# Turning the attention output of 17 chunks by way of the chip's memory in four transfers, in place of eight direct ones

## The chip, the cores and the metric

One NeuronCore of a Trainium2 chip runs the whole kernel. The metric is the device time of one execution in microseconds (us), lower is better. Every time below is from runs of the kernel before, or from the hardware profile of one of its executions.

## The reference

The kernel computes three layers one after the other. A gated linear attention over 4 sequences of 768 tokens, 8 heads of width 48, whose state runs along the tokens; a dense layer 384 to 2048 to 384 with x·sigmoid(x) between; and a layer of 8 experts in which every token goes to the one expert that its logits prefer.

```python
for t in range(S):
    state = f[:, :, t, :, None] * state + np.einsum('bhd,bhe->bhde', k[:, :, t], v[:, :, t])
    y[:, :, t] = np.einsum('bhd,bhde->bhe', q[:, :, t], state)
x = y.transpose(0, 2, 1, 3).reshape(B * S, H * D)
h = x @ w_in
x = (h * (1.0 / (1.0 + np.exp(-h)))) @ w_out
...
h = np.maximum(xe @ w1[e], 0.0)
out[mask] = gate_w[mask, None] * (h @ w2[e])
```

All inputs and outputs are f32; there are 3072 tokens of 384 values.

## The kernel before, in words

The 3072 tokens are 24 chunks of 128. The attention of a chunk is done in closed form with matmuls, and the state is carried from chunk to chunk. The chunks make nine groups of the dense layer (2, 2, six times 3, and 2 chunks): group 3 is chunks 7 to 9, group 4 chunks 10 to 12, group 5 13 to 15, group 6 16 to 18, group 7 19 to 21, group 8 22 and 23. A group has 16 slots. In slot i, `moe_h` multiplies the group's tokens with 128 columns of w_in into a bank `ph` (9 matmuls on x split into a high part `xth` and a low part `xtl`), ACT makes `se` (a tanh), DVE makes `sg` from both, and `moe_g` splits that into `gh` and `gl`; two slots later (`LAG`, L85) `moe_o` multiplies these with w_out into `px`. There are two `ph` banks, so the `ph` of slot i+2 needs the `sg` of slot i. In a group's first slot the matmuls on `xth` come ahead of those on `xtl` (L673).

The attention of later chunks is spread over the slots of the group before theirs: `s0 = pos[g, 0] - NF + r * NF // sizes[g] - ASH` (L1338) and `S1` (L80) put a chunk's six stages into slots. For the last chunk of a group of three the stage that makes `xth` and `xtl` (`x_high`, `x_low`, L642 and L647) falls into the last slot ahead of the group's own first slot.

The dense layer wants a chunk's attention output transposed, with model columns on the partitions: y as 128 partitions of 3 x 128. From chunk 4 on the attention makes it already transposed, head by head: `y_out` (L576) copies two PSUM banks into a tile `yt` of 112 partitions by 4 by 128 (two heads of 48 rows each on partitions 0 to 47 and 64 to 111, in four column blocks). `y_turn` (L590) rearranges this into the tile `y`: every 16 partitions of `y` take one head's 48 rows, three rows to a partition. For chunks 4 to 6 (`TURN`, L109), whose steps stand in the hand-written list `STEPS` (`yd:4` to `yd:6`), it writes `yt` into a scratch tensor `ys` in the chip's memory with three transfers and reads it back with a fourth. For chunks 7 to 23 it issues eight transfers of 24 KB from tile to tile, one a head. All are issued on SP (`sy.dma_start`). The buffer of `y` is single, that of `yt` one of two under the tag `am`.

From group 2 on only TensorE's order and a few other instructions are kept as written; the rest of the order on SP, ACT, DVE and POOL comes from a scheduler that works with a model of the times. SP's other transfers beside a chunk are the loads of `v`, `q`, `k` and `f` of later chunks (`load_chunk`, L207), the pair `ends` and `a_all`, and a second load of the dense weights (`in_again`, `out_again`). At the end of group 7 SP also loads the first expert's weights (`w_raw`) and the first rows of its tokens (`xe_h`), from which DVE makes the two `oi_h` (L987).

In the profile the turned `y` is read by ACT at L645 (`xth<-y`) and DVE at L649 (`xtl<-y`). In the changed file, lines after L589 are 6 lower.

Of the kernel before, what the change touches and what calls it, by code (L numbers as in the profile page):

```python
# [9 lines left out]
F32 = mybir.dt.float32  # L10
# [11 lines left out]
P = 128  # L22
# [86 lines left out]
TURN = (4, 5, 6)  # L109
# [5 lines left out]
def kernel(  # L115
# [15 lines left out]
    B, H, S, D = q.shape  # L131
# [6 lines left out]
    NPR = H // 2  # L138
    CPB = S // P
    NCH = NT // P  # L140
# [12 lines left out]
    dram = ctx.enter_context(tc.tile_pool(name="dram", bufs=1, space=DRAM))  # L153
# [10 lines left out]

    ends = dram.tile([NCH, DM], F32, name="ends")
    xs = dram.tile([E * CAP, ROW], F32, name="xs")
    ys = {n: dram.tile([NPR * P, P], F32, name=f"ys_{n}") for n in TURN}

    ident = const.tile([P, P], F32, name="ident")
    trir = const.tile([P, P], F32R, name="trir")  # L170
# [15 lines left out]
    zrow = big[:, 4 * DM : 4 * DM + ROW].bitcast(F32)  # L186
    spare = big[:, 5 * DM + 2 : 5 * DM + 3]
    BANKS = {0: "haahhaaa", 1: "-aahhaaa"}

    def turned(n):  # L190
        return n > 6 or n in TURN

    def use(n, i, name):
        if (n, i) in SPARE:
# [12 lines left out]
    def load_chunk(n, names, pin=lambda fn: fn):  # L207
        b, c = divmod(n, CPB)
        g, r = group_of[n]
        for nm in names:  # L210
            src = {"f": f_logit, "q": q, "k": k, "v": v}[nm]
            if nm == "v":
                tag, bufs = ("gl", GB) if n == 1 else ("in_v", 1)
                flat = att.tile([P, H * D + 16], F32, tag=tag, name=f"v_{n}", bufs=bufs)
                if turned(n):
                    nc.gpsimd.memset(flat[:, H * D :], 0.0)
                t = flat[:, : H * D].rearrange("p (h d) -> p h d", h=H)
                loaded[nm, n] = flat
            elif n == 1:
                tag = {"f": "sg", "q": "gh", "k": "gh"}[nm]  # L220
                t = att.tile([P, H, D], F32, tag=tag, name=f"{nm}_{n}", bufs=BUFS[tag])
            elif nm == "f":
                if n in F_HOME:
                    fb[g] = att.tile([P, 1, H, D], F32, tag=F_HOME[n], name=f"f_{n}")
                elif n == starts[g]:
                    fb[g] = att.tile([P, CPG, H, D], F32, tag="in_f", name=f"f_{n}")
                t = fb[g][:, r if g > 1 else 0]
            else:
                t = att.tile([P, H, D], F32, tag="in_" + nm, name=f"{nm}_{n}")
            (pin(nc.sync.dma_start) if not strict else sy.dma_start)(out=t, in_=src[b, :, c * P : (c + 1) * P, :].rearrange("h p d -> p h d"))  # L230
            loaded.setdefault((nm, n), t)
# [13 lines left out]
    ve, ac, sy = Pinned(nc.vector), Pinned(nc.scalar), Pinned(nc.sync)  # L245
# [300 lines left out]
    def y_past(n):  # L546
        qt = bd["qt", n]
        for i in range(NPR):
            r = (0, 2, 1, 3)[i] if turned(n) else i
            for j in range(2):  # L550
                rows = slice(64 * j, 64 * j + D)
                if turned(n):
                    pe.matmul(place(n, r, j), packed_state[rows, r, :], qt[rows, r, :], start=r % 2 == 0, stop=False)
                else:
                    pe.matmul(
                        y_banks(n)[j][:, r * D : (r + 1) * D], qt[rows, r, :], packed_state[rows, r, :D],
                        start=r == 0, stop=False,
                    )
# [31 lines left out]
    def y_turn(n):  # L590
        yt = ysb[n]
        y = ysb[n] = att.tile([P, KC, P], F32, tag="y", name=f"y_{n}")
        if n in TURN:
            rows = ys[n].rearrange("(r p) t -> p r t", r=NPR)
            sy.dma_start(out=rows[:112, :2], in_=yt[:112, :2])
            for k in range(2):
                sy.dma_start(out=rows[64 * (1 - k) : 64 * (1 - k) + D, 2:], in_=yt[64 * k : 64 * k + D, 2:])
            sy.dma_start(out=y, in_=ys[n].rearrange("(h x) t -> h x t", h=H)[:, :D])
            return
        for h in range(H):  # L600
            r, j = divmod(h, 2)
            k = j ^ r // 2
            sy.dma_start(out=y[h * P // H : (h + 1) * P // H], in_=yt[64 * k : 64 * k + D, r])

    def att4(n):
        if n % CPB:
            y_past(n)
        y_own(n)
        if n % CPB < CPB - 1:
            gain(n)  # L610
        y_out(n)
        if turned(n):
            y_turn(n)
        if n % CPB < CPB - 1:
            carry(n, bd.pop(("pu", n)), n % CPB == 0)
# [718 lines left out]
    for n in range(NCH):  # L1334
        g, r = group_of[n]
# [74 lines left out]
    def queue(early):  # L1410
# [3 lines left out]
        f=lambda n: load_chunk(n, "f"), k=lambda n: load_chunk(n, "k"), q=lambda n: load_chunk(n, "q"),  # L1414
# [5 lines left out]
        fk=lambda n: flat(n, "k"), fq=lambda n: flat(n, "q"), kt=lambda n: unflat(n, "k"), qt=lambda n: unflat(n, "q"),  # L1420
        sc=scores, am=mask, pu=gain, st=lambda n: carry(n, bd.pop(("pu", n)), n % CPB == 0), past=y_past, own=y_own,
        y=y_out, yd=y_turn, pt=flip_y, xh=x_high, xl=x_low,
        ends=lambda n: put_ends(n, queue(n == 0)), a=lambda n: spread_ends(n, queue(n == 0)),
        w=lambda n: warm(spare_bank[0], n),
# [101 lines left out]
```

## Time and profile before

| what | us |
|---|---|
| median of 3 runs | 825.18 |
| the three runs | 825.69, 819.7, 825.18 |
| the profiled execution | 824.64 |
| its span, first to last instruction | 822.9 |

The rows further down are from that one execution. Times count from the start of the span. PE is TensorE's matmul, DVE VectorE, ACT ScalarE, SPq the issuing of SyncE: the duration of an SPq row is the time to issue, not the transfer. "[2.84 <-DMA y<-yt]" behind a row is how long its engine had been idle before it and what ended that. The core's mean granted TensorE clock is 0.989 of full speed.

### The profile page before, as it was taken

How to read it: one execution, taken by the hardware profiler on the slowest of the kernel's cores; microseconds unless marked ns; L12 is line 12 of the kernel's file. 1: busy time of each engine (PE TensorE's matmuls, PEld its weight loads, DVE VectorE, ACT ScalarE, POOL GpSimd, SP SyncE). 2: the span in 40 equal slices, each digit the busy share in tenths (PEclk: the TensorE clock that was granted, in tenths of full speed). 3: DMA queues.
4: the chain of work that ended last, by engine and by line, in shares of the span. 5: the costliest groups of instructions: out<-in, count | busy, mean ns of one | idle time of the engine just before them, and what ended most of it. 6: DMA issues, size and time to landing. Idle time of an engine off the chain costs nothing.

```text
span 822.9 us, 15636 instructions
## 1 busy us (share of the span) xinstructions
PE 799.7 (97%) x5831; PEld 750.0 (91%) x5831; DVE 467.7 (57%) x1258; ACT 379.1 (46%) x838; POOL 62.4 (8%) x114
## 2 busy tenths in 40 slices
PE   7999999999999999999999999999999999999994
PEld 4889979989999999999999999999899999989994
DVE  7789986555556555646656556366573426345520
ACT  5465564453453453454345342354473526445520
POOL 2000000001000100100100101001200010111001
PEclk9799999999999999999999999999999999999998
DMA  9566686424333343343443422323380617644500
GB/s 217 150 167 161 171 242 183 112 40 116 79 87 90 92 100 83 92 107 78 107 97 79 106 58 57 119 65 119 129 278 31 205 51 259 219 151 161 172 17 29
DMA packets 173197, 100.34 MB, mean 122 GB/s; under 512 B 115507, under 2 KB 166723, under 8 KB 173110
## 3 DMA queue, kind: packets, MB, share of 16 engines
q1 hardware_dynamic: 168724, 88.56, 39.4%
q0 software_dynamic: 3280, 9.49, 3.1%
q10 hardware_dynamic: 1106, 1.18, 0.4%
q8 instruction: 48, 0.79, 0.4%
q14 instruction: 39, 0.32, 0.1%
HBM read 79.35 MB, written 16.97 MB: 117 GB/s over the span
## 4 chain that ended last, share of the span: by engine, by line
PE 78%; issue 8%; DVE 7%; DMA 2%; ACT 2%; POOL 1%; SPq 1%; POOLq 0%; ACTq 0%; DVEq 0%
PE ph L420 22%; PE px L420 21%; PE p L420 8%; PE po L420 8%; PE py L420 4%; PE sc L420 2%; DVE out_cv L248 2%; PE pyb L420 2%; DVE in_cv L248 1%; PE plt L425 1%; PE pl L420 1%; PE p_r L420 1%; POOL out_dram L988 1%; PE pq L425 1%; PE pxs L425 1%
## 5 line engine op out<-in xcount | busy, mean ns | idle before, releaser
L420 PE MATMUL px<-out_lo,gh 128*128 128x384 f32 x368 | 130.2, 354 | 0.0
L679 DVE SCALAR_TENSOR_TENSOR sg<-se,ph 128x384 f32<-128x384 f32 (+1 forms) x113 | 60.2, 532 | 116.0 <-ACT se L677 114.9
L420 PE MATMUL ph<-xth,in_lo 128*128 128x384 f32 (+1 forms) x384 | 123.9, 323 | 0.7 <-DVE sg L679 0.5
L420 PE MATMUL px<-out_hi,gl 128*128 128x384 f32 x368 | 124.0, 337 | 0.0
L420 PE MATMUL ph<-xth,in_hi 128*128 128x384 f32 (+1 forms) x384 | 123.6, 322 | 0.0
L420 PE MATMUL ph<-xtl,in_hi 128*128 128x384 f32 (+1 forms) x384 | 122.3, 325 | 1.3 <-DVE sg L248 1.2
L420 PE MATMUL px<-out_hi,gh 128*128 128x384 f32 x368 | 123.4, 335 | 0.0
L677 ACT ACTIVATE se<-ph 128x384 f32<-128x384 f32 (+1 forms) x113 | 53.6, 474 | 137.1 <-PE ph L420 131.6
L687 ACT CAST gh<-sg 128x384 fp32r<-128x384 f32 (+1 forms) x113 | 56.3, 499 | 53.1 <-DVE sg L679 50.7
L688 DVE TENSOR_TENSOR gl<-sg,gh 128x384 fp32r<-128x384 f32 (+1 forms) x113 | 60.4, 535 | 25.8 <-ACT gh L687 25.1
L420 PEld LDWEIGHTS ph<-xtl,in_hi 128*128 128x128 f32 x384 | 71.7, 188 | 3.2 <-DVE sg L248 1.9
L420 PEld LDWEIGHTS ph<-xth,in_lo 128*128 128x128 f32 x384 | 72.2, 188 | 1.5 <-DVE sg L679 0.8
L420 PEld LDWEIGHTS ph<-xth,in_hi 128*128 128x128 f32 x384 | 72.1, 188 | 0.0
L420 PEld LDWEIGHTS px<-out_lo,gh 128*128 128x128 f32 x368 | 69.1, 188 | 2.5 <-ACT gh L687 0.6
L420 PEld LDWEIGHTS px<-out_hi,gl 128*128 128x128 f32 x368 | 69.3, 188 | 0.3
L420 PEld LDWEIGHTS px<-out_hi,gh 128*128 128x128 f32 x368 | 69.1, 188 | 0.0
L420 PE MATMUL po<-w_lo,hh 128*128 128x384 f32 (+4 forms) x184 | 62.9, 342 | 0.0
L420 PE MATMUL po<-w_hi,hh 128*128 128x384 f32 (+4 forms) x184 | 61.9, 336 | 0.0
L420 PE MATMUL po<-w_hi,hl 128*128 128x384 f32 (+4 forms) x184 | 61.9, 336 | 0.0
L276 DVE TENSOR_TENSOR w_lo<-w_raw,w_hi 128x384 fp32r<-128x384 f32 x104 | 52.3, 552 | 10.8 <-ACT w_hi L275 10.7
L420 PE MATMUL p<-xsl,w_hi 128*128 128x480 f32 (+6 forms) x168 | 58.4, 347 | 0.0
L420 PE MATMUL p<-xsh,w_hi 128*128 128x480 f32 (+6 forms) x168 | 58.3, 347 | 0.0
(290 smaller groups left out, 1532.6 us busy)
## 6 DMA issues: line engine op xcount, KB each, us to landing
w_raw<-in_moe_w_dram SPq DMA_DIRECT2D x64, 384.0 KB
xs<-big SPq DMA_DIRECT2D x8, 776.0 KB
in_again<-in_moe_w_in_dram SPq DMA_DIRECT2D x16, 384.0 KB
out_again<-in_moe_w_out_dram SPq DMA_DIRECT2D x16, 384.0 KB
in_raw<-in_moe_w_in_dram SPq DMA_DIRECT2D x15, 384.0 KB
xe<-xs SPq DMA_DIRECT2D x7, 776.0 KB
out_raw<-in_moe_w_out_dram SPq DMA_DIRECT2D x14, 384.0 KB
f<-in_f_logit_dram SPq DMA_DIRECT2D x24, 192.0 KB
```

Of the source, the lines that this page charges most:

```text
L248: return lambda *a, **k: tc.keep_in_program_order(fn(*a, **k))
L276: (keep(lo_engine.tensor_sub) if pin else lo_engine.tensor_sub)(lo[:, h], x, hi[:, h].bitcast(F32))
L420: ins = nc.tensor.matmul(*a, **k)
L425: ins = nc.tensor.transpose(*a, **k)
L677: ac.activation(e, ph[:, :GT], AF.Tanh, scale=0.5)
L679: ve.scalar_tensor_tensor(out=t, in0=e, scalar=1.0, in1=ph[:, :GT], op0=ALU.add, op1=ALU.mult)
L687: ac.copy(hi, t)
L688: ve.tensor_sub(lo, t, hi.bitcast(F32))
L988: ins = nc.gpsimd.indirect_dma_start(out=out[:, :], out_offset=bass.IndirectOffsetOnAxis(ap=idx[:n], axis=0), in_=o[:n], in_offset=None, b ...
```

## The change

`y_turn` does for all chunks from 4 on what it did for chunks 4 to 6, and a scratch tensor is made for each of them.

```diff
-    ys = {n: dram.tile([NPR * P, P], F32, name=f"ys_{n}") for n in TURN}
+    def turned(n):
+        return n > 6 or n in TURN
+
+    ys = {n: dram.tile([NPR * P, P], F32, name=f"ys_{n}") for n in range(NCH) if turned(n)}
...
-
-    def turned(n):
-        return n > 6 or n in TURN
...
         y = ysb[n] = att.tile([P, KC, P], F32, tag="y", name=f"y_{n}")
-        if n in TURN:
-            rows = ys[n].rearrange("(r p) t -> p r t", r=NPR)
-            sy.dma_start(out=rows[:112, :2], in_=yt[:112, :2])
-            for k in range(2):
-                sy.dma_start(out=rows[64 * (1 - k) : 64 * (1 - k) + D, 2:], in_=yt[64 * k : 64 * k + D, 2:])
-            sy.dma_start(out=y, in_=ys[n].rearrange("(h x) t -> h x t", h=H)[:, :D])
-            return
-        for h in range(H):
-            r, j = divmod(h, 2)
-            k = j ^ r // 2
-            sy.dma_start(out=y[h * P // H : (h + 1) * P // H], in_=yt[64 * k : 64 * k + D, r])
+        rows = ys[n].rearrange("(r p) t -> p r t", r=NPR)
+        sy.dma_start(out=rows[:112, :2], in_=yt[:112, :2])
+        for k in range(2):
+            sy.dma_start(out=rows[64 * (1 - k) : 64 * (1 - k) + D, 2:], in_=yt[64 * k : 64 * k + D, 2:])
+        sy.dma_start(out=y, in_=ys[n].rearrange("(h x) t -> h x t", h=H)[:, :D])
```

On SP, at chunk 9 (the last of group 3), the eight transfers from `yt` to `y` stand before like this, with the load of a later `v` after the first:

```order
L603 DMA y_2567<-yt_2564 16x3x128
L230 DMA v_2382<-in_v_dram 128x8x48
L603 DMA y_2567<-yt_2564 16x3x128 x7
L459 DMA ends<-ep_2610 1x384
L230 DMA q_2617<-in_q_dram 128x8x48
L230 DMA k_2619<-in_k_dram 128x8x48
L463 DMA a_all<-ends 48x4x1 x2
```

and now like this, where `ys_82` is the chunk's scratch tensor:

```order
L596 DMA ys_82<-yt_2573 48x2x128
L230 DMA v_2391<-in_v_dram 128x8x48
L594 DMA ys_82<-yt_2573 112x2x128
L596 DMA ys_82<-yt_2573 48x2x128
L597 DMA y_2576<-ys_82 128x1x384
L459 DMA ends<-ep_2615 1x384
L230 DMA k_2624<-in_k_dram 128x8x48
L230 DMA q_2622<-in_q_dram 128x8x48
L463 DMA a_all<-ends 48x4x1 x2
```

The read of `ys` stands right behind the writes, ahead of `ends`, `k` and `q`; so it does at the last chunks of groups 4 to 7 and at chunk 22. At the other chunks of the groups of three it stands behind `ends` and one or both of `q` and `k`.

On SP, at chunk 23 (the last of all), the eight transfers stand before ahead of an expert weight load and of `xe_h`:

```order
L603 DMA y_6592<-yt_6589 16x3x128 x8
L248 ISA
L248 DMA w_0_1_raw_7005<-in_moe_w_dram 128x3x256
L248 ISA
L248 DMA xe_h<-xs 128x2x388
L248 ISA
```

and now the writes do, while the read stands behind both:

```order
L594 DMA ys_96<-yt_6542 112x2x128
L596 DMA ys_96<-yt_6542 48x2x128 x2
L248 ISA
L248 DMA w_0_1_raw_6954<-in_moe_w_dram 128x3x256
L248 ISA
L248 DMA xe_h<-xs 128x2x388
L597 DMA y_6545<-ys_96 128x1x384
L248 ISA
```

The load `xe_h` moved ahead by five issues, and the last part of the turn moved behind it.

On DVE, at the same place, stands before (the names are those of the slots 13 and 14 of group 7):

```order
L679 SCALAR_TENSOR_TENSOR sg_13_6669<-se_13_6667,ph_13_6657 128x384
L649 TENSOR_TENSOR xtl_6298<-y_6592,xth_6297 128x384
L688 TENSOR_TENSOR gl_13_6680<-sg_13_6669,gh_13_6679 128x384
L987 CAST oi_h_7568<-xe_h 128x1
L987 CAST oi_h_7615<-xe_h 128x1
L679 SCALAR_TENSOR_TENSOR sg_14_6704<-se_14_6702,ph_14_6692 128x384
```

and now:

```order
L673 SCALAR_TENSOR_TENSOR sg_13_6618<-se_13_6616,ph_13_6606 128x384
L981 CAST oi_h_7517<-xe_h 128x1
L981 CAST oi_h_7564<-xe_h 128x1
L682 TENSOR_TENSOR gl_13_6629<-sg_13_6618,gh_13_6628 128x384
L643 TENSOR_TENSOR xtl_6251<-y_6545,xth_6250 128x384
L673 SCALAR_TENSOR_TENSOR sg_14_6653<-se_14_6651,ph_14_6641 128x384
```

The two `oi_h` moved ahead of `gl` and `xtl`; all of them still stand ahead of the `sg` of slot 14. Elsewhere TensorE's and POOL's orders are the same as before, ACT has `xth` moved by one place at chunks 12, 17, 22 and 23, and DVE has `xtl` moved by one to five places at six chunks.

## Rows read from the trace of the kernel before

**Rows 1.** Page, part 1: busy us (share of the span) xinstructions.

```profile
PE 799.7 (97%) x5831; PEld 750.0 (91%) x5831; DVE 467.7 (57%) x1258; ACT 379.1 (46%) x838; POOL 62.4 (8%) x114
```

**Rows 2.** Busy time of each engine in the stretch of chunks 7 to 23.

```profile
145.00:530.00 385.00, 383.38 (x3032) 363.98 (x3027) 215.97 (x623) 167.72 (x348) 21.31 (x35) 1.00 0.36 90
```

**Rows 3.** Waits of PE: who, for whom, us in total, times, longest.

```profile
PE plt L425 <- ACT yt L581: 1.0, 1, 1.0
...
PE ph L420 <- DVE sg L679: 0.5, 1, 0.5
...
PE ph L420 <- ACT xth L645: 0.2, 1, 0.2
```

**Rows 4.** Instructions on the tile y: ns min/median/max, and the waits ahead of them.

```profile
L603 SPq DMA_DIRECT2D y<-yt x136: 556/591/1455, 145.7 to 520.4; - x136
...
  DMA y<-yt: 31.0, 15
```

**Rows 5.** Instructions on the tile yt: the writes into ys at chunks 4 to 6.

```profile
L248 SPq DMA_DIRECT2D ys<-yt x9: 344/472/1193, 78.2 to 119.5; - x9
```

**Rows 6.** Timeline of SP at chunk 4: start, duration, instruction.

```profile
78.19 2.46 SPq L248 DMA_DIRECT2D ys<-yt  x3
82.67 0.70 SPq L248 DMA_DIRECT2D y<-ys  x1
```

**Rows 7.** Windows after chunk 4's read: last two columns DMA share and GB/s.

```profile
82.67:85.17 2.50, 2.50 (x21) 2.29 (x19) 2.47 (x7) 0.51 (x2) 0.00 (x0) 1.00 0.22 51
85.17:85.67 0.50, 0.19 (x4) 0.07 (x4) 0.50 (x2) 0.28 (x2) 0.00 (x0) 1.00 0.99 303
```

**Rows 8.** The chain that ended last: a read of 194 KB, issue to landing.

```profile
581.80 2.48 DMA xe_r<-xs
```

**Rows 9.** Timeline at chunk 9, SP, ACT and PE: the start of group 3.

```profile
192.02 0.57 SPq L603 DMA_DIRECT2D y<-yt  x1
192.68 1.40 SPq L230 DMA_DIRECT2D v<-in_v_dram  x1
...
199.92 0.51 ACT L645 CAST xth<-y 128x384 fp32r<-128x384 f32 x1 [2.84 <-DMA y<-yt]
...
200.24 0.33 PE L420 MATMUL px<-out_hi,gh 128*128 128x384 f32 x1
...
200.48 0.45 PE L420 MATMUL ph<-xth,in_lo 128*128 128x384 f32 x1
```

**Rows 10.** Timeline at chunk 12, SP, ACT and PE: the start of group 4.

```profile
259.44 5.03 SPq L603 DMA_DIRECT2D y<-yt  x8
...
265.92 0.51 ACT L645 CAST xth<-y 128x384 fp32r<-128x384 f32 x1 [0.85 <-DMA ends<-ep]
...
266.48 0.44 PE L420 MATMUL ph<-xth,in_lo 128*128 128x384 f32 x1 [0.15 <-ACT xth L645]
```

**Rows 11.** Timeline at chunk 21, ACT and PE: the start of group 7.

```profile
464.15 0.51 ACT L645 CAST xth<-y 128x384 fp32r<-128x384 f32 x1 [2.19 <-DMA y<-yt]
...
465.37 0.34 PE L420 MATMUL ph<-xth,in_lo 128*128 128x384 f32 x1
```

**Rows 12.** Timeline at chunk 14, DVE and PE: a slot behind an xth.

```profile
314.56 0.54 DVE L679 SCALAR_TENSOR_TENSOR sg<-se,ph 128x384 f32<-128x384 f32 x1
...
316.46 0.34 PE L420 MATMUL ph<-xtl,in_hi 128*128 128x384 f32 x1
```

**Rows 13.** Timeline at chunk 23, SP, PE and DVE: the start of group 8.

```profile
515.48 5.48 SPq L603 DMA_DIRECT2D y<-yt  x8
...
522.25 0.37 SPq L248 DMA_DIRECT2D xe_h<-xs  x1
...
526.25 0.33 PE L420 MATMUL px<-out_hi,gh 128*128 128x384 f32 x1
526.36 0.21 DVE L987 CAST oi_h<-xe_h 128x1 int32<-128x1 f32 x2 [2.18 <-DMA xe_h<-xs]
...
527.09 0.39 PE L420 MATMUL ph<-xth,in_lo 128*128 128x256 f32 x1 [0.51 <-DVE sg L679]
```

## The prediction

> **What bounds the kernel now.** I read the page's busy shares first: TensorE is busy 97% of the span, no other engine over 57% [rows 1]. That is an average, so the second view is the busy time in the stretch that the change touches, chunks 7 to 23: of its 385.00 us TensorE is busy 383.38 [rows 2]. It stands still there for 1.62 us in all, and that is the most that any change of transfers in this stretch can win, unless the matmuls themselves got faster; their number and order stay. The third view says what ends these pauses [rows 3]: 1.0 us at one transpose that waits for the copies into `yt`, which come ahead of the transfers and are left as they are; 0.5 us for a `sg`; 0.2 us for an `xth`. Only the last two can hang on the turning of y.
>
> So the eight transfers are no bottleneck, although they look like one. SP spends 591 ns on each of 136 of them, and ACT stands still 31.0 us, 15 times, until they land [rows 4]. ACT is 46% busy, and its waits cost something only where TensorE reaches the product of the delayed instruction too early. The question is then not how much issue time goes, but when y lands, and what margin each chunk has.
>
> **What the change removes.** Eight issues a chunk make 8 x 0.591 = 4.7 us on SP; three writes at a median of 472 ns [rows 5] and one read at 0.70 us [rows 6] make 2.1. That is 2.6 us less on SP for each of 17 chunks, 44 us in all. I cost this at nothing: no wait of TensorE's list ends with a load on SP in this stretch [rows 3], and the loads of q, k and v are for later chunks. If that cover were gone it would be a gain, not a loss.
>
> **What the change adds: a wait on SP and a second transfer in series.** The read may be issued only when the writes have landed. At chunk 4 the last write's issue ends at 78.19 + 2.46 = 80.65 and the read's issue starts at 82.67: 2.02 us [rows 6]; I take 2.0. Chunks 5 and 6 show 1.94 and, with another issue between, 2.23. Behind the waiting read stand, at the last chunks of the groups, `ends` and the loads of k and q; they still leave SP earlier than they did.
>
> How long the read takes is not shown, since chunks 4 to 6 use y long after it lands. From below: after chunk 4's read was issued the DMA engines moved 51 GB/s for 2.50 us, 127 KB, and then 303 GB/s [rows 7]. If every byte were the read's, its 197 KB are through 70/303 = 0.23 us into the second window, so it takes 2.73 us or more. A read of nearly the same size from the chip's memory, `xe_r`, landed 2.48 us after its issue [rows 8]. From above: `xe_h`, twice the size and behind a weight load, was issued at 522.25 and used at 526.36, 4.1 us [rows 13]. I take 3.3: a little over the bound that is this very transfer, since other loads were in those bytes. The ends 2.7 and 4.1 are kept for the range.
>
> A rule of the Trainium skill speaks against this read (DMA: Bandwidth & Descriptors, section on why a DMA increments its semaphore by 16): a transfer runs on the largest number of engines up to 16 that divides the slowest dimension on both sides. If this read's slowest source dimension is the eight heads, eight engines carry it. At the page's 27 GiB/s an engine its data would take 0.85 us in place of 0.42, an estimate; with 0.4 us more the sum below would be +1.5 in place of +0.4. Rows 7 don't tell the engines apart.
>
> **Where it reaches TensorE.** The chunks that count are the last of a group, whose `xth` is wanted at once.
>
> - Chunk 9: the first write takes the place of the first transfer at 192.02, `v` ends at 194.08 [rows 9], two writes more end at about 195.1, the read goes out at 197.1 and lands at 200.4, so `xth` starts at 200.5 in place of 199.92: 0.6 later. TensorE's first matmul of group 3 started at 200.48, 0.24 after the one ahead of it where 0.17 is usual [rows 9]: it has no margin, and the 0.6 is paid in full.
> - Chunk 12: three writes from 259.44 end at 260.95, the read goes out at 262.95 and lands at 266.25; `xth` starts at 266.35 in place of 265.92 [rows 10]. TensorE waits already: 0.43 is paid.
> - Chunks 15, 18, 21: `xth` comes 0.45 to 0.67 later by the same steps. At chunk 21 it ended at 464.66 and was wanted at 465.37, a margin of 0.71 [rows 11]; the other two have 0.80 and 0.97. Nothing is paid.
> - The chunks within groups: what waits behind a late `xth` on ACT is a `se`, then `sg`, and TensorE wants that bank two slots on. The narrowest is chunk 14: `sg` ends at 315.10, the matmul that needs the bank starts at 316.46 [rows 12], a margin of 1.35 against some 0.5 later. Nothing is paid.
> - Chunk 23 gains. There DVE stood idle for `xe_h`, and the `sg` queued behind `oi_h` cost TensorE 527.09 - 526.25 - 0.17 = 0.67 us [rows 13]. Three writes end at 517.0 where the eight ended at 520.96, so `xe_h` goes out some 3.9 us earlier and lands at 522.4. The read, behind `xe_h`, lands about 1 us after it, at 523.4; `xth`, `xtl` and the `sg` take 2.2 us more to 525.6, ahead of the 526.42 at which TensorE wants it. The 0.67 goes.
>
> The sum is 0.6 + 0.43 - 0.67 = +0.4 us. Against the profiled execution, 824.64 (its span of 822.9 and 1.7 around it), that is 825.0; the median of the runs shown is 0.5 above that execution, so 825.5.
>
> With the read at 2.7 us, chunk 9 costs nothing, chunk 12 wins 0.1, and the sum is -0.8. With 4.1, the lateness grows by 0.8: chunk 9 costs 1.4, chunk 12 1.2, chunks 15, 18 and 21 about 0.5 each, the gain at chunk 23 is about gone, and the sum is +4.2.
>
> **Rivals.**
>
> 1. The two hops are no longer than eight issues, and every pause that hangs on y goes: the 0.2 of chunk 12 (0.3 with the spacing) and the 0.67, so about -1.0, 824.2 on the median's scale. For it: the issues alone take 5.5 us of a chunk [rows 13]. Against it: 2.0 and 2.7 are what two landings take at least, and the writes 1.5.
> 2. Slower: the read, not the write, is the long hop, because it comes back through queues in which v, q, k and weight loads stand, and it decides at the starts of groups 3 to 7 and in chunk 14. With y later by L, TensorE pays L at chunks 9 and 12, and L less 0.80, 0.97, 0.71 and 1.35 at chunks 15, 18, 21 and 14. With the gain at chunk 23 kept this is 6L - 4.5 once L is over 1.35. It passes 1% (8.2 us) at L = 2.1, a read of some 5 us: 833.4. For it: the 4.1 us of `xe_h`. Against: 36% mean DMA share in this stretch [rows 2].
> 3. The transfers are not what is replaced, or the freed 44 us of SP move something that I take for hidden. For the first: nothing, the issue order shows four a chunk. For the second: no row of TensorE's waits.
>
> **How the numbers follow.** My forecast, between -0.8 and +4.2 with the chunk margins as read, has 0.78; rival 1 has 0.12, rival 2 0.07, an unseen gain of over 1% 0.03. One per cent, 8.3 us, is about what a measurement of this kernel can tell from no change: the three runs alone span 6.0. So faster is 0.03, the same 0.90, slower 0.07. The range goes from 819.5, just under the fastest run shown (819.7), to 829.9, which is the sum of +4.2 on the slowest run shown (825.69).
>
> **What would show it.** The trace after should have the read's issue 2 us behind the third write's, `xth` at chunk 9 near 200.5 with TensorE's start of group 3 just behind it, margins left at groups 5 to 7, DVE's `oi_h` near 522.5, and no wait for `sg` at group 8. ACT's waits at L639 should be a little longer than the 31.0 us, not shorter. TensorE's idle time in the stretch should be 1 to 3 us. Wrong would be: idle time of TensorE over 5 us there, a read that lands under 2.5 us or over 4.5 after its issue, or any change before chunk 7 or behind the dense layer.

## The result and the profile after

| | before | after |
|---|---|---|
| median of 20 runs each | 820.88 us | 825.58 us |
| lowest and highest | 819.18, 825.69 | 822.73, 830.6 |
| ratio after / before, 95% interval | | 1.0056, 1.0039 to 1.0074 |

The change is no gain: 4.6 us slower (3.2 to 6.1 by the interval), inside the 1% that was called no change, but clear of it on the slow side. The predicted 825.5 lies beside the 825.58 for a bad reason: it stood on the median of three runs, 825.18, and twenty runs of the same kernel have 820.88. The forecast sum was +0.4 us, and that is what failed.

The two spans can't be subtracted either. TensorE's granted clock in the first 70 us, which the change does not touch, was lower in the profiled execution of before (0.93 on average, so part of the time at 1.2 GHz) than in that of after (1.00, 2.4 GHz throughout). Windows of before, with the granted clock third from the end:

```profile
0.00:70.00 70.00, 63.69 (x505) 52.21 (x505) 54.84 (x125) 39.26 (x83) 4.51 (x32) 0.93 0.72 180
...
131.36:527.09 395.73, 394.12 (x3120) 373.88 (x3119) 222.16 (x643) 171.45 (x356) 21.89 (x38) 1.00 0.37 93
```

The same windows of after:

```profile
0.00:70.00 70.00, 64.05 (x560) 53.22 (x561) 58.87 (x135) 41.56 (x90) 4.61 (x33) 1.00 0.75 190
...
125.84:525.55 399.71, 395.47 (x3121) 374.52 (x3120) 220.81 (x643) 170.69 (x356) 23.50 (x38) 1.00 0.40 101
```

The second row of each runs from the first matmul of group 2 to that of group 8, at full clock in both. I call it the stretch and compare all kernels by it, since whatever the opening does only shifts it: 395.7 us before, 399.7 after, +4.0. Of these 2.6 are idle time of TensorE (395.73 - 394.12 = 1.6 before, 399.71 - 395.47 = 4.2 after); the other 1.4 are matmuls whose starts lie further apart without a wait of PE's own. Where the idle time stands [rows 3] shows in the waits of PE after:

```profile
PE ph L420 <- ACT xth L639: 2.6, 3, 1.4
PE plt L425 <- ACT yt L581: 1.2, 1, 1.2
PE ph L420 <- DVE sg L673: 0.5, 1, 0.5
```

The 0.2 us at `xth` have become 2.6, in three places. The `sg` wait of 0.5 is still there. On ACT, the instructions on the tile `y` [rows 4] now show:

```profile
L597 SPq DMA_DIRECT2D y<-ys x17: 597/609/686, 144.4 to 520.1; - x17
...
  DMA y<-ys: 54.5, 17
```

So SP issues far less, as the change says, and ACT stands 54.5 us for y in place of 31.0. From the first issue of a chunk's y to the start of its `xth`, the median over 17 chunks is 8.12 us; before it was 7.17. Of this, the end of the last write's issue to the start of the read's takes 1.82, and the start of the read's issue to `xth` 3.83 (3.55 to 4.79).

TensorE runs the same instructions in the same order in both, so their starts can be subtracted one by one. From the first matmul of group 2 on, after falls behind by:

| place | forecast, us | measured, us |
|---|---|---|
| transposes of chunk 8's `yt` | 0 | +0.33 |
| start of group 3 (chunk 9) | +0.6 | +1.47 |
| `am` product behind chunk 11's late `xth` | 0 | +0.39 |
| start of group 4 (chunk 12) | +0.43 | +0.51 |
| `am` product near 386 | 0 | +0.19 |
| `rt` product behind chunk 19's late `xth` | 0 | +0.27 |
| chunk 21 and the start of group 7 | 0 | +0.78 |
| start of group 8 (chunk 23) | -0.67 | +0.03 |
| sum | +0.4 | +4.0 |

### The profile page after: what moved, and what is told of

Its sections match the earlier page's. It is cut to its first block, busy times and chain, and to the rows that moved or that the text cites. A ratio compares the mean times of both kernels' runs of the same rounds, so it can differ in the third digit from the quotient of the medians.

```text
span 821.2 us, 15504 instructions
## 1 busy us (share of the span) xinstructions
PE 795.8 (97%) x5831; PEld 746.6 (91%) x5831; DVE 466.7 (57%) x1258; ACT 378.1 (46%) x838; POOL 63.9 (8%) x114
## 4 chain that ended last, share of the span: by engine, by line
PE 70%; issue 8%; DVE 7%; DMA 7%; ACT 4%; SPq 1%; POOL 1%; POOLq 0%; DVEq 0%; ACTq 0%
PE ph L420 20%; PE px L420 18%; PE po L420 7%; PE p L420 7%; PE py L420 3%; PE sc L420 3%; DMA y<-ys 2%; DMA ys<-yt 2%; PE pyb L420 1%; DVE out_cv L248 1%; DMA w_raw<-in_moe_w_dram 1%; DVE in_cv L248 1%; PE pq L425 1%; PE p_r L420 1%; POOL out_dram L982 1%
```

## The experiments

Each kernel is the changed one with another `y_turn`, unless said otherwise; the scheduler orders SP, ACT and DVE anew in each, so more than the edit can move. The times, with the ratio to the kernel before in the same session (medians 819.8 and 819.57 there), and the stretch of the profiled execution:

| kernel | median, us | ratio, 95% interval | stretch, us |
|---|---|---|---|
| e1_ends_direct | 821.5 | 1.0004 (0.9971 to 1.0038) | 397.7 |
| e2_ends_memory | 823.75 | 1.004 (1.0011 to 1.0068) | 398.9 |
| e3_packed_read | 818.44 | 0.9992 (0.9964 to 1.002) | 394.85 |
| e4_old_scratch | 822.4 | 1.0018 (0.9991 to 1.0044) | 398.5 |
| e5_pitch_64 | 825.91 | 1.007 (1.0047 to 1.0092) | 402.2 |
| e6_ends_19_direct | 821.31 | 1.0012 (0.9983 to 1.004) | 396.1 |
| e7_packed_again | 818.58 | 0.998 (0.9954 to 1.0007) | 394.7 |
| e8_before_again | 820.32 | 1.0009 (0.9979 to 1.0038) | 395.4 |

Theory A: a late y is all that costs, and only where TensorE wants `xth` at once, at the starts of groups. Theory B: the added traffic and the other order cost a little everywhere. Theory C: the read is slow because of its form.

### Which chunks cost: e1 and e2

In e1 the last chunks of the groups take y directly again, in e2 only they go by memory.

```diff
     y = ysb[n] = att.tile([P, KC, P], F32, tag="y", name=f"y_{n}")
+    if n in (9, 12, 15, 18, 21, 23):        # e2: n > 6 and n not in (...)
+        for h in range(H):
+            r, j = divmod(h, 2)
+            k = j ^ r // 2
+            sy.dma_start(out=y[h * P // H : (h + 1) * P // H], in_=yt[64 * k : 64 * k + D, r])
+        return
```

> The last chunks of groups 3 to 8 (9, 12, 15, 18, 21, 23) are turned by eight direct transfers again, the eleven others by way of the chip's memory. Stretch from TensorE's first matmul on group 2 to its first on group 8: 395.7 us before, 399.7 after. Theory A (only a late y at a group's start costs TensorE): 396 to 397. Rival B (the memory traffic or the moved orders cost a little at every chunk): 11/17 of the 4.0 stays, 398.3. Theory A also has TensorE's first matmul on groups 3, 4 and 7 pause 0.3 us or less.

> The converse: only chunks 9, 12, 15, 18, 21 and 23 go by way of the chip's memory, the eleven others by eight direct transfers. Theory A: nearly all of the cost stays, 399 us or more in the stretch from group 2 to group 8 (395.7 before, 399.7 after). Rival B: 6/17 of it, 397.1.

The stretch of e1 is 397.7, between the two forecasts; that of e2 is 398.9, near A's bound. In e2, TensorE waits 2.5 us for `xth` at three group starts; in e1 this is 0.5 at one, the start of group 4, where A had 0.3 at most. The excesses of the two over before, 2.0 and 3.2, add up to more than after's 4.0, so the stretches alone don't tell A from B. And of e1's 2.0, 1.5 stand at one place in mid-group, where A had nothing. The timeline of e1 there, DVE, SP, ACT and PE:

```profile
420.47 0.56 DVE L649 TENSOR_TENSOR xtl<-y,xth 128x384 fp32r<-128x384 f32 x1 [3.49 <-ACT xth L645]
...
422.81 0.55 DVE L248 TENSOR_TENSOR lfl<-f,lfh 128x384 fp32r<-128x384 f32 x1
...
423.39 1.01 SPq L230 DMA_DIRECT2D f<-in_f_logit_dram  x2
...
427.44 0.56 DVE L392 TENSOR_SCALAR f<-f 128x768 f32<-128x768 f32 x1 [2.01 <-DMA f<-in_f_logit_dram]
...
431.34 0.24 ACT L770 COPY rt<-pg 96x128 f32<-96x128 f32 x1
...
431.64 0.33 PE L420 MATMUL pyb<-qt,state 48*64 48x128 f32 x2 [1.08 <-ACT rt L770]
```

Read it from below. TensorE waits for `rt` on ACT; ACT works through `f` and a table load ahead of it, and had waited for the load of `f`. That load left SP at 423.39, because it refills the buffer that DVE's `lfl` reads, and `lfl` stands in DVE's queue behind `xtl`, which had waited 3.49 us for chunk 19's y. So a late y is also paid inside a group, eleven microseconds later, by an instruction that never touches y.

### The form of the read: e3 and e5

In e3 the scratch is packed: 384 rows without gaps, so that the read is one run of rows, three to each partition. The writes become four. In e5 the four writes stay, but each head's 48 rows lie 64 apart again and the read has eight pieces, as in the changed kernel.

```diff
-    rows = ys[n].rearrange("(r p) t -> p r t", r=NPR)
-    sy.dma_start(out=rows[:112, :2], in_=yt[:112, :2])
-    for k in range(2):
-        sy.dma_start(out=rows[64 * (1 - k) : 64 * (1 - k) + D, 2:], in_=yt[64 * k : 64 * k + D, 2:])
-    sy.dma_start(out=y, in_=ys[n].rearrange("(h x) t -> h x t", h=H)[:, :D])
+    packed = ys[n][: H * D]
+    for b in range(2):
+        for k in range(2):
+            rows = packed.rearrange("(r j d) t -> j d r t", j=2, d=D)[k ^ b]
+            # e5: rows = ys[n].rearrange("(r j d) t -> j d r t", j=2, d=64)[k ^ b][:D]
+            sy.dma_start(out=rows[:, 2 * b : 2 * b + 2], in_=yt[64 * k : 64 * k + D, 2 * b : 2 * b + 2])
+    sy.dma_start(out=y, in_=packed.rearrange("(p c) t -> p c t", c=KC))
+    # e5: sy.dma_start(out=y, in_=ys[n].rearrange("(h x) t -> h x t", h=H)[:, :D])
```

Chunks 4 to 6 stay as they were.

> As the changed kernel, but for chunks 7 to 23 the scratch tensor is packed (384 rows, no gaps), so that the read is one plain 128 x 384 block; the writes become four of 48 x 2 x 128. In the changed kernel the turned y is used 3.8 us (median) after its read is issued. Theory C (the read is slow because its outermost source dimension of eight spreads it over half the DMA engines): 3.3 us or less, and the pauses at groups 3 and 7 shrink by 0.3 to 0.5 less what the fourth write adds. Rival D (the latency of a read from the chip's memory behind the loads on the same queues sets it): 3.6 to 3.9 us, and the pauses grow by the fourth write's 0.5.

> The packed kernel's four writes (48 rows x 2 blocks each), but each head's 48 rows again 64 rows apart in the scratch, so that the read has eight pieces as in the changed kernel; nothing else differs from the packed kernel. Theory C (it is the read's form that made it slow: eight separate pieces, so not all DMA engines carry it): the time from the read's issue to xth's start is back at 3.6 to 4.0 us (2.47 packed, 3.83 changed kernel), the time from the last write's issue to the read's stays at the packed kernel's 1.4 us, TensorE waits again at the starts of groups 3, 4 and 7 (over 0.4 us each), and the stretch from group 2's to group 8's first matmul is 398.5 to 400 us. Rival (the gain of the packed kernel came from its other writes, or from less lines touched in the chip's memory): the read takes 2.5 to 2.9 us, no waits at group starts, stretch 394.8 to 396.

| median over 17 chunks, us | after | e5 | e3 |
|---|---|---|---|
| end of the last write's issue to the read's | 1.82 | 1.43 | 1.42 |
| read's issue to `xth` | 3.83 | 3.79 | 2.47 |
| first issue to `xth` | 8.12 | 8.10 | 6.83 |

Theory C holds: with the same writes, the pieces alone make 1.3 us. In e3 the pauses at the group starts, for which 0.3 to 0.5 less was expected, are gone altogether. The four writes gain 0.4 in the wait ahead of the read and lose it to one more issue. The read itself can be seen at chunk 15, where little else moves. After the change its issue starts at 325.42; the windows behind it (last two columns DMA share and GB/s):

```profile
326.42:326.82 0.40, 0.40 (x5) 0.40 (x4) 0.40 (x2) 0.40 (x2) 0.00 (x0) 1.00 0.14 8
326.82:327.22 0.40, 0.40 (x4) 0.40 (x3) 0.40 (x2) 0.16 (x1) 0.00 (x0) 1.00 0.53 73
327.22:327.62 0.40, 0.40 (x4) 0.40 (x3) 0.40 (x2) 0.00 (x0) 0.00 (x0) 1.00 0.16 38
327.62:328.02 0.40, 0.40 (x5) 0.40 (x3) 0.40 (x2) 0.00 (x0) 0.00 (x0) 1.00 0.48 180
```

Packed (the run e7 of the same kernel), with the issue at 323.64:

```profile
324.64:325.04 0.40, 0.40 (x4) 0.40 (x4) 0.40 (x2) 0.36 (x1) 0.00 (x0) 1.00 0.66 138
325.04:325.44 0.40, 0.40 (x4) 0.40 (x3) 0.40 (x2) 0.00 (x0) 0.00 (x0) 1.00 0.90 330
325.44:325.84 0.40, 0.40 (x4) 0.40 (x3) 0.40 (x2) 0.00 (x0) 0.00 (x0) 1.00 0.03 8
```

The packed read is through 1.8 us after its issue: 0.4 x (138 + 330) makes 187 KB of its 197. The one in pieces has moved 0.4 x (8 + 73 + 38 + 180) = 120 KB at most by 2.6 us. In its fullest such window 0.48 of the engines' time carries 180 GB/s, where 0.90 carry 330: the same speed an engine, on half as many. The rule of the Trainium skill that the prediction weighed (DMA: Bandwidth & Descriptors, section on why a DMA increments its semaphore by 16) says eight engines for this read, and the rows agree; the 0.4 us estimated from its rate fall short of the 1.3 measured. The traces' semaphore updates agree too: each of the 17 reads of after and of e5 has one update 1.0 to 1.1 us after the start of its issue and eight more when it lands, each of the packed ones has sixteen when it lands.

At 330 and at 180 GB/s the 197 KB take 0.6 and 1.1 us, so the halved rate explains 0.5 of the 1.3. The packets of the reads (128 of 1536 bytes each) show where all of it lies. These are medians over 17 reads, in us; landing is the last update of the semaphore that `xth` waits for:

| after the start of the read's issue | after | e5 | e3 |
|---|---|---|---|
| first packet starts | 1.40 | 1.40 | 0.98 |
| last packet ends | 3.27 | 3.09 | 2.07 |
| landing | 3.81 | 3.77 | 2.45 |

The packets start 0.4 us later, behind an issue that is itself 0.27 longer; they take 0.6 to 0.8 longer; and the landing follows the last of them after 0.2 to 0.3 more. Why the start and the end are later too stays open, and so does what the gaps would cost with all engines at work: a read in pieces with another leading dimension was not run.

What a late y costs is seen in the waits of PE in the stretch of e5, the worst kernel, whose last chunks and inner chunks both pay:

```profile
PE ph L420 <- ACT xth L646: 2.4, 3, 0.9
PE pyb L420 <- ACT rt L771: 1.6, 1, 1.6
PE ph L420 <- DVE sg L680: 0.9, 1, 0.9
PE plt L425 <- ACT yt L581: 0.9, 1, 0.9
PE pg L420 <- ACT rt L757: 0.5, 1, 0.5
```

For e5 I expected a stretch of at most 400 us; it is 402.2. Its three waits at group starts are those of the forecast. What I had left out is again in mid-group: 1.6 and 0.5 for `rt`, 0.9 for an `sg`.

### Taking the wait out by an older scratch: e4

```diff
-    sy.dma_start(out=y, in_=ys[n].rearrange("(h x) t -> h x t", h=H)[:, :D])
+    sy.dma_start(out=y, in_=ys[n if n in TURN else n - 1].rearrange("(h x) t -> h x t", h=H)[:, :D])
```

> As the changed kernel, but for chunks 7 to 23 the read takes the scratch tensor of the chunk before, so that the output of those chunks is that of the chunk before; all transfers stay. The read then has nothing fresh to wait for and y is there many us ahead of its use. Theory A: every pause that hangs on y goes, 395.0 to 395.6 us in the stretch from group 2 to group 8 (395.7 before, 399.7 after). Rival B: the traffic stays, so most of the cost stays, 398 or more.

This kernel turns the output of the chunk before, so its numbers are those of other data. It did not do what it was to do. No group start waits for `xth`, as A has it, but the stretch is 398.5, as B has it. The trace shows neither: reads moved forward took `xth` and `xtl` forward with them in the order of ACT and DVE, and those still stand and wait. The timeline at chunk 7, SP, ACT and PE:

```profile
128.36 0.62 SPq L597 DMA_DIRECT2D y<-ys  x1
...
132.97 0.51 ACT L639 CAST xth<-y 128x384 fp32r<-128x384 f32 x1 [5.63 <-DMA y<-ys]
...
134.59 0.44 PE L420 MATMUL ph<-xtl,in_hi 128*128 128x384 f32 x1 [1.47 <-DVE sg L673]
```

This `xth` serves only the next group, yet TensorE pays 1.47 us, for an `sg` that stands on DVE right behind chunk 7's `xtl`. It doesn't tell A from B, but shows the second way of paying by itself.

### The widened theory, and the two kernels once more: e6, e7, e8

Theory A was widened: a late y is paid at group starts, and within groups by what stands behind `xth` and `xtl` on ACT and DVE. e6 is e1 with chunk 19 direct too; e7 is e3 again, e8 the kernel before again.

```diff
-    if n in (9, 12, 15, 18, 21, 23):
+    if n in (9, 12, 15, 18, 19, 21, 23):
```

> As the kernel with the last chunks of the groups direct, with chunk 19 (within its group) direct too. Theory A, widened (a late y is also paid inside a group, by what stands in order behind xth and xtl on ACT and DVE: in that kernel chunk 19's late xtl held up lfl on DVE, hence the load of f, hence the product rt, for which TensorE waited 1.1 us at 431): that pause is gone or under 0.3 us, and the stretch from group 2's to group 8's first matmul is 396.0 to 396.6 us in place of 397.73. Rival B (the added traffic slows loads everywhere): the load of f stays late or another pause takes its place, stretch 397.4 or more.

> The packed kernel once more, in more rounds, to tell whether it beats the kernel before. If the stretch decides: 394.6 to 395.2 us for it (394.85 the first time, 395.73 before), so about 0.7 us less than before, a ratio of 0.9985 to 0.9998. Rival: the first result was chance of the opening, ratio 1.000 or more, stretch 395.5 or more.

> The kernel before, unchanged, as a measure of what two runs of one kernel differ by, and for a second trace of it. If the opening's clock only shifts everything behind it: stretch from group 2's to group 8's first matmul 395.5 to 396.0 us whatever the opening, ratio 1.000 within 0.002. Rival: the stretch itself scatters by over 0.5 us, and then differences of that size between kernels mean nothing.

The waits of PE in the stretch of e6:

```profile
PE plt L425 <- ACT yt L581: 1.2, 1, 1.2
PE ph L420 <- DVE sg L679: 0.3, 1, 0.3
```

The pause for `rt` is gone and none takes its place: 396.06 us, as expected, with ten chunks still going by memory. Over the kernels, what TensorE loses at this place goes, within some 0.2 us, with how late chunk 19's `xth` is (against before, with TensorE's own shift taken off): 0.5 us late and nothing lost in e8, 0.7 and 0.27 in after, 0.85 and 0.15 in e6, 0.95 and 0.5 in e2, 2.0 and 1.5 in e1, 2.4 and 2.0 in e5. In e6 and e2 chunk 19 is turned directly, so it is when y lands that counts, by whichever way. Traffic as such (theory B) costs no more than the 0.3 to 0.6 us by which this lies over the two stretches of before, and the packed kernel, with all seventeen, is below before. In that one, e7, only the wait that comes ahead of the transfers is left:

```profile
PE plt L425 <- ACT yt L581: 0.9, 1, 0.9
```

e8 answers what differences mean: 395.44 against 395.73, though group 2 begins 4.8 us later in it. It also has 1.3 us at the `plt` where before had 1.0, so after's +0.33 there is scatter. The packed kernel's 394.85 and 394.7 are 0.6 to 1.0 below the two stretches of before, which is the `sg` of chunk 23 and, against the first of them, the pause of chunk 12 (e8 has none there). In whole runs its ratio, 0.998 (0.9954 to 1.0007), doesn't separate it from before; from the changed kernel's 1.0056 (1.0039 to 1.0074) it does.

## Why the prediction was right or wrong

**What bounds the kernel: right.** TensorE sets the time, and nothing came back for the 44 us of freed issue; what counted was when y lands.

**The wait from write to read: right.** 2.0 was taken, 1.82 measured. At chunk 9 the read was to go out at 197.1. TensorE ran 5.5 us earlier in after and had lost 0.3 again by then, so that is 191.9, and it left at 191.88. Rows of chunk 9 [rows 9], SP, ACT and PE, after:

```profile
187.25 1.78 SPq L230 DMA_DIRECT2D v<-in_v_dram  x1
189.13 0.53 SPq L594 DMA_DIRECT2D ys<-yt  x1
189.70 0.45 SPq L596 DMA_DIRECT2D ys<-yt  x1
191.88 0.61 SPq L597 DMA_DIRECT2D y<-ys  x1
...
196.21 0.51 ACT L639 CAST xth<-y 128x384 fp32r<-128x384 f32 x1 [4.32 <-DMA y<-ys]
...
196.77 0.45 PE L420 MATMUL ph<-xth,in_lo 128*128 128x384 f32 x1 [1.38 <-ACT xth L639]
```

**The read, "I take 3.3": mis-sized.** With 0.1 to `xth` it should have been 3.4; here it is 196.21 - 191.88 = 4.33, and all of the extra 0.9 us at chunk 9 is this. The step that failed is the nearness of the bound: chunk 4's read gave 2.73 "or more" by bytes, and I put the landing close over it. The bytes are through about when taken, 3.45 us after the issue at chunk 9 and 3.27 in the median; but the semaphore is complete only at 4.30 and 3.81. That the trace of before does not show how long the read takes was wrong too: its semaphore updates have it. Those of the reads of chunks 4 to 6, which have the same eight pieces, are complete 4.42, 4.55 and 5.37 us after the start of the issue, with more traffic beside them (DMA share 0.67 there) but all above the upper end of 4.1. `xe_r`, a read of nearly the same size, had landed in 2.48 [rows 8], but it is not this read. The upper end, 4.1, was the better guess; its sum of +4.2 lies beside the measured 4.0, though partly by other terms.

**Chunk 12: right in place, low by 0.1.** Rows [rows 10] after: the read took 263.12 - 259.09 = 4.03 in place of 3.4, and 0.39 of that lateness was covered by what TensorE had already lost at the `am`.

```profile
259.09 0.60 SPq L597 DMA_DIRECT2D y<-ys  x1
...
263.12 0.51 ACT L639 CAST xth<-y 128x384 fp32r<-128x384 f32 x1 [3.68 <-DMA y<-ys]
...
263.68 0.44 PE L420 MATMUL ph<-xth,in_lo 128*128 128x384 f32 x1 [0.67 <-ACT xth L639]
```

**Chunks 15, 18 and 21, "nothing is paid": right for the first two, wrong at 21.** There the wait and the read were both slower than taken (2.22 and 3.84), `xth` came 1.3 us later, and the margin of 0.71 [rows 11] became a wait:

```profile
463.13 0.51 ACT L639 CAST xth<-y 128x384 fp32r<-128x384 f32 x1 [3.52 <-DMA y<-ys]
...
463.70 0.44 PE L420 MATMUL ph<-xth,in_lo 128*128 128x384 f32 x1 [0.51 <-ACT xth L639]
```

**"The chunks within groups. Nothing is paid": wrong.** I followed ACT's `se` and DVE's `sg` behind a late `xth`, and at chunk 14 the margin held. I didn't follow the rest of DVE's queue: `am`, and `lfl`, on which the load of `f` hangs. Chunk 11 pays 0.39 by it in after, where its late `xth` has `am` 2.1 us late; chunk 19 pays 0.27 in after, no more than the scatter between the two traces of before, but 1.5 in e1, and e6 shows that this goes with the lateness of that one chunk.

**Chunk 23, "xe_h goes out some 3.9 us earlier": wrong.** SP was free for it, but `xe_h` reads `xs`, and the scatter into `xs` hadn't landed. The wait of SP's queue between 513 and 521, and the rows of SP, DVE, ACT and PE [rows 13]:

```profile
SPq L248 <- DMA xs<-x,r_idx: 2.8, 1, 2.8
```

```profile
518.65 0.40 SPq L248 DMA_DIRECT2D xe_h<-xs  x1
520.14 0.69 SPq L597 DMA_DIRECT2D y<-ys  x1
...
522.02 0.21 DVE L981 CAST oi_h<-xe_h 128x1 int32<-128x1 f32 x2 [3.64 <-DMA xe_h<-xs]
...
523.92 0.51 ACT L639 CAST xth<-y 128x384 fp32r<-128x384 f32 x1 [5.00 <-DMA y<-ys]
...
524.95 0.55 DVE L673 SCALAR_TENSOR_TENSOR sg<-se,ph 128x384 f32<-128x384 f32 x1
...
525.55 0.39 PE L420 MATMUL ph<-xth,in_lo 128*128 128x256 f32 x1 [0.52 <-DVE sg L673]
```

The wait stands in SP's queue ahead of the read, so the read went out at 520.14, 5.75 us behind the last write. Before, `oi_h` was late and held up `sg`; now y is late and holds up `sg`. The stall kept its place and its size, and changed its cause.

**The rivals.** Rival 1 (every pause goes, -1.0) did not happen here, but the packed kernel is it: its hops are no longer than eight issues, and it wins the 0.7 of chunk 23 and the pause of chunk 12. Rival 2 had the place right, a read that is the long hop, at a lateness of about 1 us in place of 2.1; its reason, the loads in the same queues, is not what sets the read's time, since in e3 and e5 much the same loads stand there and the form makes the difference. Rival 3 fell: e6 and the packed kernel free SP's time as well and lose nothing clear by it.

**The signs.** TensorE's idle time, 1 to 3 us expected, is 4.2 (over 5 would have been "wrong"); the longest read, at chunk 16, lands at 4.76 and so passes the 4.5 that was named as a sign of being wrong; group 7 has no margin left, group 8 still waits for `sg`, and ACT's waits are not a little longer than 31.0 but 54.5.

## What to carry over

A wait for data costs what is queued behind it, so follow the whole queue of each engine that stands, and the buffers that its instructions free, until the next product that TensorE wants; a margin at the first consumer is not the chunk's margin. Before a round trip through memory takes the place of direct transfers, lay the scratch out so that the read is one run of rows with a leading dimension that spreads over all engines: with the writes alike, that is here the difference between 6.4 us lost (e5) and 0.6 to 1.0 us gained (e3, e7) in the stretch, a gain that whole runs don't separate from nothing. And take the base of an absolute time from many runs; the median of three was 4.3 us off.

## What was unexpected of the hardware

A read of 197 KB from the chip's memory took 3.8 us to its first use in eight pieces 32 KB apart and 2.5 us in one run, with the same bytes and the same writes ahead; its issue on SP shrank with it, from a median of 609 ns to 344. And the granted clock of the opening, between 0.88 and 1.00 in the first 70 us of the profiled executions, put the first matmul of group 2 anywhere from 125.8 to 136.2, while the stretch behind it kept its length within 0.3 us in the two traces of the unchanged kernel.
